# Norm factors by a block-diagonal matmul, and a gated-convolution loop interleaved slice by slice

## Chip, core and metric

The kernel runs on one core of a Trainium2 chip. The metric is device time in microseconds (us) of one execution. Beside it stands one profiled execution, whose trace gives the duration of every instruction and what each engine waited for.

## What is computed

```python
B, H, S, D = 8, 8, 576, 64          # DM = H * D = 512
kv  = einsum('bhsd,bhse->bhde', k, v)
out = einsum('bhsd,bhde->bhse', q, kv)
x   = out / sqrt(mean(out * out, -1) + 1e-6) * g_norm      # per head, 64 values
x   = x.transpose(0, 2, 1, 3).reshape(B, S, DM)
x1, x2, x3 = split(x @ w_proj, 3)                          # w_proj: 512 x 1536
x2  = irfft(rfft(x2, axis=1) * rfft(filter_fft, axis=0))   # along S, 576 long
result = (x1 * x2 * x3) @ w_out                            # 8 x 576 x 512, float32
```

## The kernel before

Everything is held transposed: the 512 channels lie on partitions as four **slices** of 128 (two heads each), the 576 rows of a batch along the free axis, as two halves of 288. Matmul operands are bf16, sums fp32.

The Fourier transforms are matmuls by tables that the kernel makes at its start (`ang`, `IV`, `FW`, `FWr`). The 576 rows are folded into three blocks of 192: `rr` is their sum, `ab` two differences. One transform of a batch is three groups: g = 0 on the sum (97 frequencies), g = 1 (128), and g = 2 (a middle piece). The transformed filter lies in `HH` and `HM`.

The work of one batch is written as functions:

- `kv(b)`: 40 matmuls for the k-v products of all heads, copied into `kvblk`; `qtr(b)`: 36 transposes of q, copied into `qT`.
- `att_o(b, j)`: two matmuls give slice j of the attention output. ScalarE (ACT) squares it into `sq`, and copies it times `g_norm` into `osb` (in batch 0 VectorE, DVE, does the copy).
- `att_r(b)`: eight matmuls by `ind_sq`, 32 columns wide, add the squares per head for all four slices into one tile; ACT makes Ln and Exp(-0.5 ...) of it, one each of 128x576, in `rstd`.
- `att_x(b, jp)`: matmuls by `ind_bc` spread the factors of a pair of slices over the 64 rows of each head, and DVE multiplies them from PSUM into `x`.
- `fold(b)`: three DVE operations over all four slices give `rr` and `ab`.
- `proj2(b)`: the x2 projection out of `rr` and `ab`; ACT copies it to `x2`.
- `fft(b)`: the three groups of the transform. DVE multiplies g = 0 and g = 1 twice each with `HH` (into `tpw`, 1024 elements), GpSimd (POOL) adds them into `Y`; g = 2 takes one DVE multiplication.
- `proj13(b, dc)`: sixteen matmuls for slice dc of x1 and x3. ACT copies x1, DVE multiplies x3 by it into `g13`.
- `invc`, `inv`: the inverse transform, folded; DVE combines its parts in four operations a pair of slices and multiplies with `g13` into `yg`.
- `outp(b)`: the output projection, copied by ACT and sent by DMA. The last 64 rows of two batches share a tile, so its third part runs for odd b only.

PSUM is one pool of four tiles (`psp`, bufs=4) of two banks each; every result above takes one. Most tiles in SBUF have one buffer: `x`, `ab`, `rr`, `qT`, `Y`, `g13`. Input loads are issued on POOL's queue, the filter and the outputs on SyncE's (SP's).

The order of the loop was: `proj2(b)`, `kv(b+1)`, `qtr(b+1)`, `fft(b)`, four times [`proj13(b, dc)`, `att_o(b+1, dc)`], `att_r(b+1)`, `outp(b-1)`, `att_x(b+1)`, `fold(b+1)`, `invc(b)`, `inv(b)`. A scheduler puts the instructions of each engine in a fixed order near to this one when the program is built; each engine then runs its own list in order and waits where an operand or a tile is not ready. Memsets without `tc.keep_in_program_order` may be put at any earlier place.

Of the kernel before, what the change touches and what calls it, by code (L numbers as in the profile page):

```python
# [20 lines left out]
def kernel(  # L21
# [26 lines left out]

    consts = ctx.enter_context(tc.tile_pool(name="consts", bufs=1))
# [64 lines left out]
    def load_filter():  # L114
        f4 = moe_filter_fft.rearrange("(m p c) d -> c p m d", m=3, c=3)
        lo, hi = slice(0, 64), slice(64, 128)
        for o, i in ((fa[lo, 0:3], f4[0]), (fa[hi, 0:3], f4[1]), (fa[lo, 3], f4[2][:, 1]), (fc[lo, 0], f4[2][:, 0]),
                     (fc[lo, 1], f4[2][:, 2]), (fc[hi, 0:2], f4[0][:, 1:3]), (fc[lo, 2:4], f4[1][:, 1:3]),
                     (fc[hi, 2:4], f4[2][:, 1:3])):
            nc.sync.dma_start(out=o, in_=i)  # L120
# [9 lines left out]
    for c, tag in enumerate(("x", "Y", "g13")):  # L130
# [9 lines left out]
        if c == 1:  # L140

            for t in (fa, fc):
                tc.keep_in_program_order(nc.vector.memset(t[:, :, 0:1], 0.0))
            load_filter()
# [14 lines left out]
    nc.vector.memset(bias_eps, 1e-6)  # L159


    ind_sq = consts.tile([P, 32], BF16)
    nc.vector.memset(ind_sq, 0.0)
    nc.vector.memset(ind_sq[0:64, 0:1], 1.0)
    nc.vector.memset(ind_sq[64:128, 1:2], 1.0)
    ind_bc = consts.tile([P, P], BF16)
    nc.vector.memset(ind_bc, 0.0)
    for j in range(4):
        nc.vector.memset(ind_bc[32 * j:32 * j + 2, 64:128], 1.0)
        nc.vector.memset(ind_bc[32 * j:32 * j + 1, 64:128], 0.0)  # L170
        nc.vector.memset(ind_bc[32 * j:32 * j + 1, 0:64], 1.0)
# [4 lines left out]
    def zeros(i):  # L176
        for t in kvt[i]:
            nc.vector.memset(t[TAIL:P], 0.0)
        nc.vector.memset(kvblk[i], 0.0)
# [68 lines left out]
    def att_r(b):  # L248
        s = st[b]
        r2 = ps_tile("ps_r2")  # L250
        for h in range(2):
            for j in range(NDC):
                nc.tensor.matmul(r2[32 * j:32 * j + 32, h, 0:TH], ind_sq, s['sq'][:, j, h * TH:(h + 1) * TH], start=True, stop=True)
        lr = work.tile([P, 2, TH], FP32, name="lr", tag="lr")
        nc.scalar.activation(out=lr, in_=r2[:, :, 0:TH], func=AF.Ln, scale=1.0 / D, bias=bias_eps)
        s['rstd'] = work.tile([P, 2, TH], BF16, name="rstd", tag="rstd")
        nc.scalar.activation(out=s['rstd'], in_=lr, func=AF.Exp, scale=-0.5)

    def att_x(b, jp):
# [3 lines left out]
        bc = [ps_tile("ps_bc") for _ in range(2)]  # L263
        for h in range(2):
            for i in range(2):
                r = slice(32 * (2 * jp + i), 32 * (2 * jp + i) + 32)
                nc.tensor.matmul(bc[i][:, h, 0:TH], ind_bc[r], s['rstd'][r, h], start=True, stop=True)  # L267
        for i in range(2):
            j = 2 * jp + i
            nc.vector.tensor_mul(out=s['x'][:, j].rearrange("p (a b) -> p a b", a=2), in0=bc[i][:, :, 0:TH],  # L270
                                 in1=s['o'][:, j].rearrange("p (a b) -> p a b", a=2))

    def fold(b):
        s = st[b]
        x3 = s['x'].rearrange("p j (m r) -> p j m r", m=3)
        ab = work.tile([P, NDC, 2, SB], BF16, name="ab", tag="ab")
        s['ab'] = ab.rearrange("p j a r -> p j (a r)")
        t_ = work.tile([P, NDC, SB], BF16, name="x01", tag="x01")
        s['rr'] = work.tile([P, NDC, SB], BF16, name="rr", tag="rr")
        nc.vector.tensor_add(out=t_, in0=x3[:, :, 0], in1=x3[:, :, 1])  # L280
        nc.vector.tensor_add(out=s['rr'], in0=t_, in1=x3[:, :, 2])
        nc.vector.tensor_sub(out=ab, in0=x3[:, :, 0:2, :], in1=x3[:, :, 2:3, :].to_broadcast([P, NDC, 2, SB]))
# [7 lines left out]
    def fold_filter():  # L290
        ff = hst['ff'] = work.tile([P, NSC, DM], BF16, name="ff", tag="x2")
        nc.vector.memset(ff[64:P, 1], 0.0)
# [9 lines left out]
        nc.vector.memset(asc, 2.0 / S)  # L302
        nc.vector.memset(asc[0:1, 0:1], 1.0 / S)
        nc.vector.memset(asc[96:97, 0:1], 1.0 / S)
# [45 lines left out]
    def fft(b):  # L350
        x2 = st[b]['x2']
        Y = work.tile([P, 6, DM], BF16, name="Y", tag="Y")
        st[b]['Y'] = Y
        for g in range(2):
            n = N1 if g == 0 else P
            ks = (0, 1) if g == 0 else (2, 3, 4)
            xp = ps_tile("ps_X")
# [7 lines left out]
        xp = ps_tile("ps_X")  # L365
# [56 lines left out]
    def outp(b):  # L422
        yg = yt[b % 2] = st[b]['yg']
        for c0 in (0, 2, 4):
            if c0 == 4 and b % 2 == 0:
                continue
# [13 lines left out]
            nc.scalar.copy(out=ot[:, 0:n], in_=pp[:, 0:n])  # L440
            for i in range(2):
                eng = nc.scalar if b == B - 1 and i else nc.sync
                if n == 2:
                    eng.dma_start(out=o_rows(b, 2 * c0 + i, 2 * c0 + 2 + i), in_=ot[64 * i:64 * i + 64])
                else:
                    eng.dma_start(out=o_rows(b - 1 + i, NR - 1), in_=ot[64 * i:64 * i + 64, 0])
# [3 lines left out]
    qtr(0)  # L450
    tables()
    for j in range(NDC):
        att_o(0, j)
    att_r(0)
    att_x(0, 0)
    att_x(0, 1)
    fold(0)
    fold_filter()
    for g in range(3):
        gen_h(g)  # L460
    zeros(1)
    for b in range(B):
# [5 lines left out]
        fft(b)  # L468
# [3 lines left out]
        for dc in range(NDC):  # L472
            proj13(b, dc)
# [45 lines left out]
```

## Time and profile before

| what | value |
|---|---|
| median of 3 runs | 278.64 us (277.81 to 281.88) |
| the profiled execution | 279.41 us, of which the span of its instructions is 277.6 us |
| granted TensorE clock, mean | 0.981 |
| busy: PE (TensorE) / DVE / ACT / POOL | 83% / 65% / 48% / 29% of the span |
| first matmul of batch 0's projection, of batch 1's, of batch 7's | 35.70, 67.12, 239.35 us |

The kernel is fully unrolled, so a batch can be read off the time line. In what follows "chain" is the chain of work that ended last, followed back from the end of the program; "groups" are instructions gathered by line and shape, with their number, total busy time, mean ns, and the idle time of the engine ahead of them with what ended it.

### The profile page before, as it was taken

How to read it: one execution, taken by the hardware profiler on the slowest of the kernel's cores; microseconds unless marked ns; L12 is line 12 of the kernel's file. 1: busy time of each engine (PE TensorE's matmuls, PEld its weight loads, DVE VectorE, ACT ScalarE, POOL GpSimd, SP SyncE). 2: the span in 40 equal slices, each digit the busy share in tenths (PEclk: the TensorE clock that was granted, in tenths of full speed). 3: DMA queues.
4: the chain of work that ended last, by engine and by line, in shares of the span. 5: the costliest groups of instructions: out<-in, count | busy, mean ns of one | idle time of the engine just before them, and what ended most of it. 6: DMA issues, size and time to landing. Idle time of an engine off the chain costs nothing.

```text
span 277.6 us, 4744 instructions
## 1 busy us (share of the span) xinstructions
PE 230.8 (83%) x1942; PEld 132.6 (48%) x1965; DVE 181.4 (65%) x283; ACT 133.6 (48%) x197; POOL 79.6 (29%) x80
## 2 busy tenths in 40 slices
PE   0227599959999899989998999999989999999690
PEld 0124125735575456545664556445744574466320
DVE  7909924739772998279936993499549952994520
ACT  1494255662367245834384437542773277233221
POOL 8722244800570058002910292003300230032000
PEclk9999999997999999999999999999999999999977
DMA  4999999990392529360985098510031002300506
GB/s 50 176 253 255 199 191 191 192 104 2 40 188 32 153 28 187 43 190 7 159 94 151 2 160 97 144 45 2 2 89 63 2 0 71 121 0 2 151 4 185
DMA packets 46231, 27.96 MB, mean 101 GB/s; under 512 B 22210, under 2 KB 40642, under 8 KB 46210
## 3 DMA queue, kind: packets, MB, share of 16 engines
q0 software_dynamic: 39744, 16.26, 48.5%
q1 hardware_dynamic: 6098, 10.75, 13.3%
q10 hardware_dynamic: 368, 0.66, 0.7%
q8 instruction: 15, 0.25, 0.3%
q14 instruction: 6, 0.05, 0.1%
HBM read 34.47 MB, written 9.44 MB: 158 GB/s over the span
## 4 chain that ended last, share of the span: by engine, by line
PE 68%; DVE 19%; issue 5%; DMA 3%; ACT 2%; ACTq 0%; SPq 0%; DVEq 0%
PE ps_x L379 22%; PE ps_out L432 10%; PE ps_x L346 8%; DVE x L270 6%; PE ps_X L360 6%; DMA fa<-in_moe_filter_fft_dram 3%; PE ps_qT L226 3%; DVE tpw L363 3%; PE ps_x L334 3%; PE ps_o L240 2%; PE ps_kv L211 2%; PE ps_inv L404 2%; PE ps_x L338 2%; PE ps_X L367 2%; PE ps_out L436 2%
## 5 line engine op out<-in xcount | busy, mean ns | idle before, releaser
L379 PE MATMUL ps_x<-x,wp 128*128 128x288 bf16 x512 | 67.5, 286 | 4.4 <-DVE tpw L363 4.4
L379 PEld LDWEIGHTS <-wp 128*128 128x128 bf16 x512 | 50.0, 98 | 19.8 <-issue 5.7
L364 POOL TENSOR_TENSOR Y<-tpw 97x1024 bf16<-97x1024 f32 (+1 forms) x16 | 37.6, 2358 | 72.7 <-DVE tpw L363 72.7
L270 DVE TENSOR_TENSOR x<-ps_bc,osb 128x576 bf16<-128x576 f32 x32 | 22.0, 749 | 30.2 <-PE ps_bc L267 30.2
L385 DVE TENSOR_TENSOR g<-ps_x,x 128x576 bf16<-128x576 f32 x32 | 24.0, 754 | 25.7 <-PE ps_x L379 25.7
L383 ACT CAST x<-ps_x 128x576 bf16<-128x576 f32 x32 | 20.4, 639 | 41.6 <-PE ps_x L379 41.6
L432 PE MATMUL ps_out<-wo,yg 128*128 128x512 bf16 x120 | 30.7, 389 | 2.8 <-DVE yg L413 2.4
L82 POOL DMA_DIRECT2D km<-in_k_dram x8 | 7.4, 924 | 82.9 <-PE ps_qT L226 78.0
L241 ACT ACTIVATE sq<-ps_o 128x576 bf16<-128x576 f32 x32 | 20.7, 650 | 17.5 <-PE ps_o L240 17.4
L440 ACT COPY ot<-ps_out 128x1024 f32<-128x1024 f32 (+1 forms) x20 | 18.3, 922 | 15.7 <-PE ps_out L432 14.9
L404 PE MATMUL ps_inv<-IV,Y 128*128 128x384 bf16 x128 | 23.4, 339 | 0.0
L346 PE MATMUL ps_x<-wp,ab 128*128 128x512 bf16 x96 | 22.1, 380 | 0.0
L229 DVE COPY qT<-ps_qT 128x512 bf16<-128x512 bf16 (+1 forms) x32 | 13.2, 452 | 12.4 <-PE ps_qT L226 11.9
L340 ACT CAST x<-ps_x 128x1024 bf16<-128x1024 f32 x8 | 8.1, 1015 | 27.1 <-PE ps_x L338 27.1
L246 ACT ACTIVATE osb<-ps_o,g_col 128x576 bf16<-128x576 f32 x28 | 20.6, 734 | 0.0
L432 PEld LDWEIGHTS <-yg 128*128 128x128 bf16 x128 | 11.5, 99 | 17.8 <-issue 3.0
L362 DVE TENSOR_TENSOR tpw<-ps_X,HH 97x1024 f32<-97x1024 f32 (+1 forms) x16 | 19.5, 1219 | 0.2
L363 DVE TENSOR_TENSOR tpw<-ps_X,HH 97x1024 f32<-97x1024 f32 (+1 forms) x16 | 19.4, 1213 | 0.0
L409 DVE TENSOR_TENSOR u<-ps_inv,cs 128x768 bf16<-128x768 f32 x16 | 15.2, 949 | 4.7 <-PE ps_inv L404 4.7
L360 PE MATMUL ps_X<-x,FW 128*128 128x512 bf16 (+1 forms) x57 | 17.9, 389 | 0.4
L226 PE MATMUL ps_qT<-ident,qb 128*64 128x128 bf16 x288 | 11.9, 232 | 6.3 <-DVE qT L229 4.0
L211 PE MATMUL ps_kv<-vm,km 128*64 128x64 bf16 x256 | 6.9, 203 | 12.2 <-DMA vm<-in_v_dram 12.2
(143 smaller groups left out, 321.9 us busy)
## 6 DMA issues: line engine op xcount, KB each, us to landing
out_dram<-ot SPq DMA_DIRECT2D x30, 256.0 KB, 3.4
qb<-in_q_dram POOLq DMA_DIRECT2D x16, 288.0 KB, 8.5
km<-in_k_dram POOLq DMA_DIRECT2D x8, 512.0 KB, 6.2
vm<-in_v_dram POOLq DMA_DIRECT2D x8, 512.0 KB, 8.1
wp<-in_moe_w_proj_dram POOLq DMA_DIRECT2D x3, 512.0 KB, 18.6
out_dram<-ot SPq DMA_DIRECT2D x7, 128.0 KB, 3.5
fa<-in_moe_filter_fft_dram SPq DMA_DIRECT2D x2, 384.0 KB, 8.2
fc<-in_moe_filter_fft_dram SPq DMA_DIRECT2D x3, 256.0 KB, 10.9
```

What stands on the lines that cost most here:

```text
L241: nc.scalar.activation(out=s['sq'][:, j].rearrange("p (a b) -> p a b", a=2), in_=op[:, :, 0:TH], func=AF.Square)
L246: nc.scalar.activation(out=o_, in_=op[:, :, 0:TH], func=AF.Copy, scale=g_col)
L270: nc.vector.tensor_mul(out=s['x'][:, j].rearrange("p (a b) -> p a b", a=2), in0=bc[i][:, :, 0:TH], in1=s['o'][:, j].rearrange("p (a b) -> ...
L346: nc.tensor.matmul(pp[:, cc], ab[:, j, (c0 + cc) * P:(c0 + cc + 1) * P], wp[:, j, DM:2 * DM], start=(j == 0), stop=(j == NDC - 1))
L360: nc.tensor.matmul(xp[:n, ri], FWr[:, ri, 0:n] if c == 1 else FW[:, a, 2 * g + ri, 0:n], x2[:, c], start=(a == 0), stop=(a == len(ks) - 1))
L363: nc.vector.tensor_mul(out=t_[:n, 1], in0=xp[:n], in1=HH[:n, g, 0:2])
L364: nc.gpsimd.tensor_add(out=Y[:n, 2 * g:2 * g + 2], in0=t_[:n, :, 0], in1=t_[:n, :, 1])
L379: nc.tensor.matmul(pp[:, h, 0:TH], w_, x[:, j, h * TH:(h + 1) * TH], start=(j == 0), stop=(j == NDC - 1))
L383: nc.scalar.copy(out=x1, in_=pp[:, :, 0:TH])
L385: nc.vector.tensor_mul(out=st[b]['g13'][:, dc].rearrange("p (a b) -> p a b", a=2), in0=pp[:, :, 0:TH], in1=x1)
L404: nc.tensor.matmul(ip[:, i, 0:2 * SB], Y[:, g, d_], IV[:, g, 0:2 * SB], start=(g == 2), stop=(g == 5))
L432: nc.tensor.matmul(pp[:, cc], yg[:, dc, c * P:(c + 1) * P], wo[:, dc], start=(dc == 0), stop=(dc == NDC - 1))
```

## The change

- `att_r` now runs per slice: two matmuls by a full 128x128 block-diagonal matrix `ind` give each row's sum already spread over its head's 64 rows. ACT takes Ln per slice and Exp per pair of slices, and `rstd` has the full 128x4x576 shape in SBUF. The matmuls of `att_x` are gone; its DVE multiplication takes both operands from SBUF, 1152 elements at a time.
- `fold` works on a pair of slices, so six DVE operations instead of three.
- The loop over slices now holds one transform group (in the order g = 1, 0, 2), `att_o`, `proj13`, `att_r`, and after each second slice `att_x` and `fold`. `outp(b-1)` follows after all of it.
- The first of `outp`'s copies goes to DVE.
- The last batch has its own ending, `last`: the inverse transform in one piece by six table rows (48 matmuls of 288 columns), one DVE multiplication a slice, and the output projection summed up slice by slice in three PSUM tiles.
- At the start: the sine table set of ACT is loaded first; the filter's load is issued in another place; batch 0's attention is slice by slice; `gen_h` runs inside batch 0, behind `kv(1)` and `qtr(1)`; most memsets keep their program order.

```diff
+    nc.scalar.preload_act_table_set("trig_and_small")
...
     def load_filter():
+        for t in (fa, fc):
+            tc.keep_in_program_order(nc.vector.memset(t[:, :, 0:1], 0.0))
...
+    ind = consts.tile([P, P], BF16)
+    tc.keep_in_program_order(nc.vector.memset(ind, 0.0))
+    for h in range(2):
+        tc.keep_in_program_order(nc.vector.memset(ind[64 * h:64 * h + 64, 64 * h:64 * h + 64], 1.0))
...
-    def att_r(b):
+    def att_r(b, j):
...
         for h in range(2):
-            for j in range(NDC):
-                nc.tensor.matmul(r2[32 * j:32 * j + 32, h, 0:TH], ind_sq, s['sq'][:, j, h * TH:(h + 1) * TH], start=True, stop=True)
...
+            nc.tensor.matmul(r2[:, h, 0:TH], ind, s['sq'][:, j, h * TH:(h + 1) * TH], start=True, stop=True)
+        nc.scalar.activation(out=s['lr'][:, j % 2].rearrange("p (a b) -> p a b", a=2), in_=r2[:, :, 0:TH], func=AF.Ln,
+                             scale=1.0 / D, bias=bias_eps)
+        if j % 2:
+            nc.scalar.activation(out=s['rstd'][:, j - 1:j + 1], in_=s['lr'], func=AF.Exp, scale=-0.5)
...
+        r = slice(2 * jp, 2 * jp + 2)
+        nc.vector.tensor_mul(out=s['x'][:, r], in0=s['o'][:, r], in1=s['rstd'][:, r])
...
+            if c0 == 0:
+                nc.vector.tensor_copy(out=ot, in_=pp)
+            else:
+                nc.scalar.copy(out=ot[:, 0:n], in_=pp[:, 0:n])
...
+    def last(b):
...
+        for dc in range(NDC):
+            ip = ps_tile("ps_inv")
+            for g in range(6):
...
+                    nc.tensor.matmul(ip[:, h, 0:TH], Y[:n, g, dc * P:(dc + 1) * P], IV[:n, g, h * TH:(h + 1) * TH],
+                                     start=(g == 0), stop=(g == 5))
...
+            if dc:
+                part(dc - 1)
+        part(NDC - 1)
+        for c in range(NSC):
...
+                (nc.scalar if i else nc.sync).dma_start(out=o_rows(bb, blk), in_=ot[64 * i:64 * i + 64, 0])
...
     kv(0)
     qtr(0)
+    load_filter()
     tables()
...
-        fft(b)
+        if b == 0:
+            for g in (1, 0, 2):
+                gen_h(g)
...
         for dc in range(NDC):
+            if dc < 3:
+                fft(b, (1, 0, 2)[dc])
+            if nxt:
+                att_o(b + 1, dc)
             proj13(b, dc)
             if nxt:
-                att_o(b + 1, dc)
-        if nxt:
-            att_r(b + 1)
+                att_r(b + 1, dc)
+                if dc % 2:
+                    att_x(b + 1, dc // 2)
+                    fold(b + 1, dc // 2)
         if b:
-            outp(b - 1)
+            for c0 in (0, 2, 4):
+                outp(b - 1, c0)
             del st[b - 1]
-        if nxt:
-            att_x(b + 1, 0)
-            att_x(b + 1, 1)
-            fold(b + 1)
+        if not nxt:
+            last(b)
+            continue
         invc(b)
```

How the order of instructions moves is seen at three places. In the lists a name's end number is one tile's; `ps_x` is the tile of a projection, `ps_r` of `att_r`, `ps_X` of a transform group, `ps_o` of `att_o`.

First TensorE in the loop over slices, batch 1. Before, all transform groups come first, and a slice is x1, x3, then the next batch's attention:

```order
L367 MATMUL ps_X<-x_725,FW 128x512
...
L379 MATMUL ps_x_871<-x,wp 128x288
...
L379 MATMUL ps_x_882<-x,wp 128x288
...
L240 MATMUL ps_o<-qT,kvblk_174 128x288
...
L379 MATMUL ps_x_899<-x,wp 128x288
```

Of the change, the same place one batch later:

```order
L353 MATMUL ps_X<-x_1062,FW 128x512
...
L233 MATMUL ps_o<-qT,kvblk_152 128x288
...
L372 MATMUL ps_x_1201<-x,wp 128x288
...
L372 MATMUL ps_x_1212<-x,wp 128x288
...
L250 MATMUL ps_r_1224<-sq,ind 128x288
...
L353 MATMUL ps_X<-x_1062,FW 97x512
```

A slice now takes five PSUM tiles of the four: a transform, the attention, x1, x3, and the sum of squares; the next transform stands behind them.

Second ScalarE in two slices of the same loop. Before, Ln (L255) and Exp (L257) stand behind the fourth slice:

```order
L383 CAST x_934<-ps_x_925 128x576
L241 ACTIVATE sq<-ps_o 128x576
L246 ACTIVATE osb<-ps_o,g_col 128x576
L383 CAST x_960<-ps_x_951 128x576
L241 ACTIVATE sq<-ps_o 128x576
L246 ACTIVATE osb<-ps_o,g_col 128x576
L255 ACTIVATE lr<-ps_r_977,bias_eps 128x576
L257 ACTIVATE rstd<-lr 128x576
```

Of the change:

```order
L234 ACTIVATE sq<-ps_o 128x576
L239 ACTIVATE osb<-ps_o,g_col 128x576
L376 CAST x_1210<-ps_x_1201 128x576
L251 ACTIVATE lr<-ps_r_1224,bias_eps 128x576
L234 ACTIVATE sq<-ps_o 128x576
L239 ACTIVATE osb<-ps_o,g_col 128x576
L376 CAST x_1251<-ps_x_1242 128x576
L251 ACTIVATE lr<-ps_r_1263,bias_eps 128x576
L254 ACTIVATE rstd<-lr 128x1152
```

Each slice now has a Ln, each second one an Exp twice as long, ahead of the next slice's square.

Third the start. VectorE before: the filter's tiles are touched (L143, after which SP issues the filter's load) between the angle computations, and its first use (L294) stands ahead of the copies of q:

```order
L137 TENSOR_TENSOR ang<-ang 128x576 x2
L143 MEMSET fa 128x4
L143 MEMSET fc 128x4
L134 TENSOR_SCALAR ang<-tv,kcol 128x576
L135 TENSOR_SCALAR ang<-ang 128x576
L136 TENSOR_SCALAR ang<-ang 128x576
L137 TENSOR_TENSOR ang<-ang 128x576
L294 TENSOR_TENSOR t_349<-fa 128x512
L229 COPY qT<-ps_qT 128x4x2x64 x2
```

Of the change:

```order
L171 MEMSET kt_83 64x256
L171 MEMSET vt_84 64x256
L172 MEMSET kvblk_151 128x256
L222 COPY qT<-ps_qT 128x4x2x64 x2
L222 COPY qT<-ps_qT 128x5x2x64 x2
L118 MEMSET fa 128x4
L118 MEMSET fc 128x4
L186 COPY FW<-ps_ft 128x640
```

The copies of q no longer stand behind the filter, and the filter's load is behind them. On TensorE the first k-v products of batch 1 now stand inside batch 0's x2 projection, where they came behind all of it before:

```order
L326 MATMUL ps_x_349<-wp,rr 128x512
...
L338 MATMUL ps_x_369<-wp,ab 128x512
...
L204 MATMUL ps_kv<-vm_82,km_81 64x64
...
L338 MATMUL ps_x_359<-wp,ab 128x512
...
L330 MATMUL ps_x_349<-wp,rr 64x512
```

So whatever holds up batch 1's k or v now also holds the rest of that projection.

132 lines of the change are left out of this document (65 added, 67 removed).

## Prediction

> **What bounds the kernel now.** I read the page first, then the span cut at the first projection matmul of batches 0, 1 and 7, then the chain and the time line of one middle batch.
>
> ```profile
> PE 230.8 (83%) x1942; PEld 132.6 (48%) x1965; DVE 181.4 (65%) x283; ACT 133.6 (48%) x197; POOL 79.6 (29%) x80
> ```
>
> ```profile
> 67.55:95.77 28.22, 26.44 (x235) 15.47 (x238) 19.28 (x27) 14.83 (x22) 9.36 (x8) 1.00 0.67 101
> ...
> 35.70:67.55 31.85, 28.01 (x235) 16.39 (x239) 17.51 (x24) 16.50 (x27) 12.27 (x12) 0.95 1.19 142
> 239.79:277.60 37.81, 27.79 (x157) 14.83 (x158) 18.56 (x25) 10.30 (x13) 4.67 (x2) 0.91 0.21 63
> ```
>
> Columns: length, then busy time of PE, PEld, DVE, ACT, POOL, the granted clock, the DMA share. There are three parts: a start of 35.7 us, seven like batches, and a last batch of 37.8. In a middle batch PE is busy 26.4 of 28.2 us, DVE 19.3, ACT 14.8: PE is the bound, and a gain can come only from PE's waits, the start and the end. The chain shows where PE waits (start, length, what):
>
> ```profile
> 75.92 0.43 PE ps_X L367 x2
> ...
> 78.00 1.14 DVE tpw L363
> ...
> 81.55 1.96 PE ps_x L379 x16
> ...
> 85.96 0.23 PE ps_r L253 x3
> ...
> 86.94 0.35 PE ps_r L253 x5
> 87.29 2.91 PE ps_out L432 x13
> 90.20 0.40 PE ps_bc L267 x6
> ...
> 95.77 0.59 PE ps_x L334 x2
> ```
>
> ```profile
> 91.64 0.83 PE L392 MATMUL ps_c<-IV,Y 97*128 97x192 bf16 x8
> 92.31 2.77 PE L404 MATMUL ps_inv<-IV,Y 128*128 128x384 bf16 x16
> ```
>
> First wait: the gate matmuls wait for the transforms' tiles; the group row of L379 below has 4.4 us over seven batches, 0.63 each. Second: the output ends at 90.20, the broadcast matmuls take 0.40, yet `invc` (L392) begins at 91.64: 1.04. Third: `inv` ends at 95.08, but the projection runs freely only from 95.77, since `rr` is late: some 0.6. With 0.2 of small change that is **2.5 us a batch**; 25.7 are work.
>
> **The steady batches.** The rows that I use (mean ns; idle time ahead, with what ended it):
>
> ```profile
> L379 PE MATMUL ps_x<-x,wp 128*128 128x288 bf16 x512 | 67.5, 286 | 4.4 <-DVE tpw L363 4.4
> L432 PE MATMUL ps_out<-wo,yg 128*128 128x512 bf16 x120 | 30.7, 389 | 2.8 <-DVE yg L413 2.4
> ...
> L270 DVE TENSOR_TENSOR x<-ps_bc,osb 128x576 bf16<-128x576 f32 x32 | 22.0, 749 | 30.2 <-PE ps_bc L267 30.2
> L241 ACT ACTIVATE sq<-ps_o 128x576 bf16<-128x576 f32 x32 | 20.7, 650 | 17.5 <-PE ps_o L240 17.4
> L246 ACT ACTIVATE osb<-ps_o,g_col 128x576 bf16<-128x576 f32 x28 | 20.6, 734 | 0.0
> L383 ACT CAST x<-ps_x 128x576 bf16<-128x576 f32 x32 | 20.4, 639 | 41.6 <-PE ps_x L379 41.6
> L413 DVE TENSOR_TENSOR yg<-u,g 128x1152 bf16<-128x1152 bf16 x16 | 12.1, 758 | 0.5
> L362 DVE TENSOR_TENSOR tpw<-ps_X,HH 128x1024 f32<-128x1024 f32 x8 | 9.7, 1214 | 0.0
> L348 ACT CAST x<-ps_x 128x1024 bf16<-128x1024 f32 x8 | 8.1, 1018 | 5.7 <-PE ps_x L346 5.7
> L255 ACT ACTIVATE lr<-ps_r,bias_eps 128x576 f32<-128x576 f32 x8 | 5.9, 740 | 1.1 <-PE ps_r L253 0.7
> L257 ACT ACTIVATE rstd<-lr 128x576 bf16<-128x576 f32 x8 | 5.5, 682 | 0.3
> L280 DVE TENSOR_TENSOR x<-x 128x768 bf16<-128x768 bf16 x8 | 4.4, 556 | 0.2
> ```
>
> PE loses `ind_sq` (0.23 + 0.35) and `ind_bc` (0.40), 0.98; it gains eight full matmuls of 288 columns at 1.96/16 = 0.122, also 0.98. Net nothing.
>
> DVE loses four multiplications of 0.749 and gets two of 1152 elements; L413 has that shape and type at 0.758: minus 1.5. Halving `fold` adds three instructions; a half costs more than half of L280's 0.556 and less than all of it, 0 to 0.8 in all, I take 0.4. The output copy is not in the trace on DVE: above 0.4 (two copies of q, 512 columns each, take 0.75 at 21.84 below), and by L362 about 1.2; I take 1.2. DVE stays near 19.4.
>
> ACT gets three more Ln (2.2), and two Exp of 1152 elements for one of 576: each between 0.68 and 1.36, by L348's 1.018 for 1024 1.15, so plus 1.6; it loses one copy, 1.0. ACT goes to about 17.7 of 26, but most of it stands in the slice loop, so I walk that loop. PE per slice: a transform of 6, 4, 3, 0 matmuls at 0.215 (L367), attention 0.25, x1 and x3 1.96, squares 0.25: 3.76, 3.3, 3.1, 2.46, together 12.6. DVE per slice: two multiplications of 1.21 and one of 0.75, 3.2, in slices 0 and 1; less in 2 and 3. ACT: 0.65 + 0.73 + 0.64 + 0.74 = 2.8, and 3.9 where an Exp follows.
>
> So DVE just keeps up, and ACT falls behind once. Counted from the loop's first matmul, PE ends slice 1 at 7.1 and slice 2 at 10.2. ACT's Ln and Exp of slice 1 (L251, L254) end at 9.1; queued behind them are the square, the scaled copy and the x1 cast of slice 2, which end near 9.75, 10.5 and 11.1. Slice 3 on PE takes over the tiles that the copy and the cast give back: it waits 0.3 for the one and, after its attention, 0.3 for the other. I charge **0.5** new wait a batch. The bounds: 0, if ACT makes it up, since in L383's row it has 41.6 us of waiting for PE over the run; 2.4, if ACT sets the pace throughout (rival B).
>
> Do the three old waits go? Transforms lie 3 us apart now, and the tile of one is needed five tiles later, when its 2.4 us of DVE are over. The broadcast tiles are gone. `rr`: `x` has one buffer, so DVE's first `x` of batch b+1 waits for the last x3 matmul of b, and behind it queue the last gate product, both folds, the second `x` and the output copy: 0.76 + 0.75 + 1.25 + 0.76 + 1.2 + 1.25 = 6.0. In that time PE has 0.25 of squares, 3.5 of output (16 at 0.224), 3.3 of `invc` and `inv`: 7.0. Covered with 1 us left; if that cover were gone, `rr` would be late again. In batch 0, without output, 0.45 is late. Saved per batch 2.5 - 0.5 = 2.0; from 67.55 to 239.79 are six batches: **12.0 us**.
>
> **The start.**
>
> ```profile
> 5.17 0.13 DVE L122 CAST kcol<-ki 128x3 f32<-128x3 int32 x1
> 10.71 0.68 ACT L138 ACTIVATE ang<-ang 128x576 f32<-128x576 f32 x1 [8.68 <-DVE ang L137]
> 11.39 1.97 SPq L120 DMA_DIRECT2D fa<-in_moe_filter_fft_dram  x3
> 11.41 1.28 ACT L146 ACT_TABLE_LOAD   x1
> 14.49 0.88 POOL L82 DMA_DIRECT2D vm<-in_v_dram  x1 [0.46 <-DMA qb<-in_q_dram]
> 20.59 0.74 ACT L215 CAST kvblk<-ps_kv 64x256 bf16<-64x256 f32 x2
> 21.84 0.75 DVE L229 COPY qT<-ps_qT 128x512 bf16<-128x512 bf16 x2
> ```
>
> ```profile
> vm<-in_v_dram POOLq DMA_DIRECT2D x1, 512.0 KB, 23.9
> ```
>
> Memsets held the first cast until 5.17; behind the tables, they free up to 2.8 us, and the table load of 1.28 goes: `kvblk` is ready near 17.2 instead of 21.3. The copies of q no longer wait for the filter. Batch 0's attention begins about 4 us earlier, near 20, and its first pair of slices is folded near 27. But batch 1's v, issued at 14.49, landed 23.9 later, at 38.4 (last row: size, us to landing), and the new order has the first k-v products of batch 1 inside this projection: PE stops there. The loads are one stream and DMA is full (share 1.19 in batch 0's row), and the filter's bytes, issued near 19.8 instead of 11.4, landing some 10 us after, go through the same engines before 38, so v comes no later and hardly earlier. From 38.4: 2.8 for the rest of the projection, 0.6 k-v, 1.1 transposes, 3.5 filter transform (ten full matmuls at 0.224, twelve half ones at 0.1), and a slow clock:
>
> ```profile
> 62.19 1.23 PE ps_c L392 x8
> 63.42 3.87 PE ps_inv L404 x16
> ```
>
> ```profile
> 63.40:67.30 3.90, 3.90 (x18) 1.99 (x16) 3.84 (x7) 0.80 (x1) 0.00 (x0) 0.68 0.00 0
> ```
>
> The chain has DVE and ACT ahead of 62.19: PE had waited for the factors and then for `x`, 2.4 us in two pieces. Then it was granted 0.68, and `inv` took 3.87 us (from 63.42) where a batch later it takes 16 x 0.164 = 2.62: 1.25 lost. I charge this once, since PE idles some 8 us before 38.4. Then 47.7 for the first transform, 12.6 + 0.5 slices, 3.3 + 0.45: batch 1's projection at 64.6 instead of 67.1: **2.5 us**. Bounds: 0 (1.3 if the clock is slow twice as long), and 6 if v lands early.
>
> The Trainium skill, TensorE: Matmul & The Clock Gate, "HAM oscillation", puts the drop to half clock at gaps of more than about 3.4 us. By it the clock would have stayed up at 63; the row shows a drop after shorter gaps, and the measurement decides. By Part 1 of that page, half rate for a window of 3.4 us costs 1.7, so the sum below would be 0.45 longer.
>
> **The last batch.**
>
> ```profile
> 263.45 1.55 PE ps_out L432 x4
> ...
> 269.32 0.72 ACTq L444
> ...
> 271.08 0.59 ACT ot L440
> ```
>
> `last` does the inverse in 48 matmuls at 0.122, 5.9, for 3.3 now: plus 2.6. The wait for `yg` that ends at 263.45 (2.4 in L432's row) goes, since each slice's product lies under the next slice's matmuls. At the end ACT copied, issued (269.32), and after its last copy (271.08, 0.59) issued once more, to 272.4: 4.1 us from the end of PE's work at 268.3. Now it copies three times 0.59 and issues five DMAs at 0.72, 5.4, of which 0.8 lie beside the last matmuls: 4.6. Sum **plus 0.7** (2.6 - 2.4 + 0.5), within 2 either way.
>
> **Sum.** 12.0 + 2.5 - 0.7 = 13.8 off. The profiled execution took 279.41 (span 277.6), so 265.6; it lies 0.8 above the median of 278.64, from which I count: 264.8.
>
> **Rivals.**
> B, ACT paces the slices: slices with an Exp take 3.9 + 0.4 of hand-overs, the others 2.8 + 0.4: 15.0 instead of 12.6. Five tiles a slice out of four make PE wait for whichever reader is late. The 2.5 us are then spent again: 28.1 a batch, 277. For it: Ln and Exp stand ahead of each next square. Against: slices 0 and 2 leave ACT 1.0 and 0.3 of slack, and the last one has the output behind it. Halfway, 271. The Trainium skill, Perfetto Trace Analysis, "Identifying Performance Opportunities", reads a gap repeating on the saturated engine as too little PSUM; before, the 0.63 of L379 recurs in seven batches, as it says; the change keeps four tiles.
> C, the start stays: the filter, issued 8 us later, holds the folds and the filter transform until 42, so batch 1 starts as now: 267.
> D, slower: each transform's tile is needed before DVE is through. One exposed multiplication of 1.21 in three slices and one Exp of 1.15 make 4.8 new waits for 2.5 old: plus 2.3 in seven batches, 295. It decides from 0.63 a slice on. For it: DVE needs 3.2 of a slice's 3.3; against: the tile is taken up again five tiles later.
> E, v lands early and no new wait remains: 12 + 3 (six batches without the 0.5) + 6 (the start's bound) - 0.7 off, 258.
>
> **Chances.** Forecast 0.57 (259 to 269), B 0.17, C 0.10, D 0.08, E 0.08. The range leaves out D, the far end of B and of E: 257 to 273. A measurement here tells 2%, 5.6 us, from no change. Faster by more (below 273): forecast, C, E and a third of B, 0.80; within: 0.12; slower: 0.08.
>
> **What would show it.** Right: middle batches of 26.2 us, no wait of a projection for `rr`, PE stopping at batch 1's first k-v until about 38, PE waits of 0.2 to 0.4 at slice 3 ended by ACT. Wrong: PE idle in each slice ahead of attention or x1 (B), ended by DVE's `tpw` (D); filter folds later than 42 (C). The forecast rests most on the four PSUM tiles being given back as I walked it, and on the landing of batch 1's v.

## The result and the profile after

The changed kernel took 268.98 us (median of 4 runs, 268.52 to 269.72) against 279.49 for the kernel before beside it: ratio 0.962, with an interval of 0.954 to 0.97. It is faster, by 10.5 us of the 13.8 that were forecast. Its profiled execution took 268.72, with a span of 267.0 (277.6 before). The ratios here and below are taken without the few executions that were slower as a whole, so a ratio need not be the quotient of two medians.

The same three views as before: the page's busy times; then the span by stages (length, then busy time of PE, PEld, DVE, ACT, POOL, the granted clock, the DMA share); then the chain of a middle batch (start, length, what).

```profile
PE 223.7 (84%) x1895; PEld 137.4 (51%) x1925; DVE 179.1 (67%) x283; ACT 150.6 (56%) x220; POOL 80.3 (30%) x80
```

```profile
68.22:228.43 160.21, 156.41 (x1375) 97.57 (x1398) 122.73 (x185) 104.95 (x153) 46.89 (x36) 1.00 0.53 85
121.82:147.89 26.07, 25.55 (x228) 16.13 (x229) 20.20 (x31) 17.17 (x25) 9.36 (x8) 1.00 0.73 108
228.43:267.00 38.57, 29.22 (x182) 17.07 (x183) 18.33 (x23) 7.83 (x11) 4.71 (x2) 0.95 0.29 80
```

Two of the rows above are cut at 228.43, where the chain has the last batch's first projection matmul; the matmul begins at 228.27. Counted from first matmul to first matmul in both kernels (67.12 and 239.35 before, 68.22 and 228.27 now), the stretch from batch 1's projection to batch 7's was 172.2 us and is 160.1: **12.2 less, 12.0 forecast**. Every second batch also has the third part of the output, which makes it 1.0 longer (28.2 and 29.2 before, 26.1 and 27.2 now). The row of one batch above has none of it, like the row ahead of the prediction: 26.07 for 28.2, where 26.2 was forecast, and ACT busy 17.17, where 17.7 was. The last batch has 38.7 for 38.3. What is missing lies ahead of 68.22, where batch 1 now starts; it started at 67.12 before, and 64.6 was forecast. The three parts, 12.2 - 0.5 - 1.1, are the 10.6 between the spans.

```profile
108.99 0.99 PE ps_x L372 x8
...
110.61 0.63 ACT osb L239
111.24 0.54 ACT x L376
...
111.82 2.12 PE ps_x L372 x16
...
119.39 2.60 PE ps_inv L397 x16
121.99 0.86 PE ps_x L326 x4
```

The chain leaves TensorE once in the batch, at slice 3, where ACT's scaled copy and x1 cast come late. `inv` runs straight into the next projection at 121.99; no broadcast and no `rr` stand between.

The start, from the chain of the same run and its stages:

```profile
15.04 24.93 DMA vm<-in_v_dram
...
40.10 0.43 PE ps_kv L204 x8
...
51.34 1.40 PE ps_X L353 x6
```

```profile
28.00:40.00 12.00, 1.48 (x4) 0.30 (x2) 7.17 (x15) 0.00 (x0) 2.24 (x3) 0.50 1.41 214
40.10:44.00 3.90, 3.90 (x18) 1.19 (x19) 0.00 (x0) 0.61 (x1) 1.49 (x2) 0.50 1.52 195
```

TensorE does 1.48 us of work in the twelve before v lands (its last wait, for v alone, is 10.6), and then 3.9 us at a granted clock of 0.50. The first transform runs at 51.34; 47.7 was forecast.

### The profile page after: what moved, and what is told of

Its sections match the earlier page's. It is cut to its first block, busy times and chain, and to the rows that moved or that the text cites. A ratio compares the mean times of both kernels' runs of the same rounds, so it can differ in the third digit from the quotient of the medians.

```text
span 267.0 us, 4694 instructions
## 1 busy us (share of the span) xinstructions
PE 223.7 (84%) x1895; PEld 137.4 (51%) x1925; DVE 179.1 (67%) x283; ACT 150.6 (56%) x220; POOL 80.3 (30%) x80
## 4 chain that ended last, share of the span: by engine, by line
PE 71%; DMA 13%; ACT 6%; DVE 4%; POOL 2%; issue 2%; ACTq 0%; POOLq 0%
PE ps_x L372 21%; DMA vm<-in_v_dram 9%; PE ps_out L423 9%; PE ps_X L353 6%; PE ps_x L338 6%; PE ps_inv L397 6%; DMA qb<-in_q_dram 3%; PE ps_qT L219 3%; PE ps_inv L459 2%; PE ps_x L326 2%; PE ps_o L233 2%; PE ps_r L250 2%; PE ps_X L360 2%; ACT osb L239 2%; PE ps_kv L204 2%
## 5 line engine op out<-in xcount | busy, mean ns | idle before, releaser
L357 POOL TENSOR_TENSOR Y<-tpw 128x1024 bf16<-128x1024 f32 (+1 forms) x16 | 37.8, 2361 | 74.7 <-DVE tpw L356 74.7
L251 ACT ACTIVATE lr<-ps_r,bias_eps 128x576 f32<-128x576 f32 x32 | 23.7, 745 | 6.5 <-PE ps_r L250 5.5
L355 DVE TENSOR_TENSOR tpw<-ps_X,HH 128x1024 f32<-128x1024 f32 (+1 forms) x16 | 19.6, 1224 | 9.4 <-PE ps_X L353 9.4
L423 PE MATMUL ps_out<-wo,yg 128*128 128x512 bf16 x106 | 25.0, 379 | 0.3
L338 PE MATMUL ps_x<-wp,ab 128*128 128x512 bf16 x90 | 23.8, 403 | 0.8 <-DVE ab L273 0.4
L204 PEld LDWEIGHTS <-km 128*64 128x64 bf16 x256 | 6.2, 119 | 26.4 <-issue 18.0
L356 DVE TENSOR_TENSOR tpw<-ps_X,HH 128x1024 f32<-128x1024 f32 (+1 forms) x16 | 19.4, 1215 | 0.0
L397 PE MATMUL ps_inv<-IV,Y 128*128 128x384 bf16 x112 | 19.4, 326 | 0.0
L261 DVE TENSOR_TENSOR x<-osb,rstd 128x1152 bf16<-128x1152 bf16 x16 | 12.1, 756 | 10.2 <-PE ps_x L372 9.9
L254 ACT ACTIVATE rstd<-lr 128x1152 bf16<-128x1152 f32 x16 | 18.6, 1165 | 0.5
L353 PE MATMUL ps_X<-x,FW 128*128 128x512 bf16 (+1 forms) x58 | 17.7, 381 | 0.2 <-ACT x L340 0.2
L402 DVE TENSOR_TENSOR u<-ps_inv,cs 128x768 bf16<-128x768 f32 x14 | 13.4, 954 | 6.2 <-PE ps_inv L397 6.2
```

The costliest lines, as they stand in the source:

```text
L251: nc.scalar.activation(out=s['lr'][:, j % 2].rearrange("p (a b) -> p a b", a=2), in_=r2[:, :, 0:TH], func=AF.Ln, scale=1.0 / D, bias=bias_eps)
L338: nc.tensor.matmul(pp[:, cc], ab[:, j, (c0 + cc) * P:(c0 + cc + 1) * P], wp[:, j, DM:2 * DM], start=(j == 0), stop=(j == NDC - 1))
L353: nc.tensor.matmul(xp[:n, ri], FWr[:, ri, 0:n] if c == 1 else FW[:, a, 2 * g + ri, 0:n], x2[:, c], start=(a == 0), stop=(a == len(ks) - 1))
L355: nc.vector.tensor_mul(out=t_[:n, 0], in0=xp[:n], in1=HH[:n, g, 1:3])
L357: nc.gpsimd.tensor_add(out=Y[:n, 2 * g:2 * g + 2], in0=t_[:n, :, 0], in1=t_[:n, :, 1])
L397: nc.tensor.matmul(ip[:, i, 0:2 * SB], Y[:, g, d_], IV[:, g, 0:2 * SB], start=(g == 2), stop=(g == 5))
```

## The experiments

Each run is compared with the kernel before; its median lay between 279.0 and 279.5 in all of them. The stages come from each run's profiled execution: the first matmul of batch 2's projection, the time from there to batch 7's (five batches), and from there to the end.

| kernel | median, us | ratio, interval | batch 2 starts | five batches | last batch |
|---|---|---|---|---|---|
| before | 279.49 | | 95.32 | 144.0 | 38.3 |
| changed | 268.98 | 0.962, 0.954 to 0.97 | 94.67 | 133.6 | 38.7 |
| norm factors only | 282.61 | 1.0136, 1.0096 to 1.0177 | 98.67 | 143.9 | 38.4 |
| order only | 267.34 | 0.9588, 0.9546 to 0.9629 | 89.99 | 138.2 | 37.1 |
| filter and projection first | 262.52 | 0.941, 0.9382 to 0.9438 | 88.37 | 133.6 | 38.7 |
| filter loaded early | 268.22 | 0.9586, 0.9533 to 0.9638 | 94.51 | 133.6 | 38.7 |
| wo last | 266.73 | 0.9569, 0.9537 to 0.9601 | 92.10 | 133.6 | 38.7 |
| five output buffers | 267.91 | 0.96, 0.9575 to 0.9626 | 95.03 | 133.6 | 38.1 |
| Exp later | 267.32 | 0.9589, 0.9557 to 0.9622 | 95.04 | 132.3 | 38.7 |
| first start and end together | 262.51 | 0.9408, 0.9387 to 0.9429 | 89.24 | 133.6 | 38.0 |
| end by two engines | 268.63 | 0.9666, 0.9606 to 0.9726 | 94.74 | 133.6 | 38.7 |
| best | 260.27 | 0.9356, 0.9272 to 0.9439 | 88.37 | 132.3 | 38.7 |
| old end | 268.08 | 0.9638, 0.9569 to 0.9707 | 94.25 | 133.6 | 39.1 |
| filled gap | 265.99 | 0.953, 0.9514 to 0.9545 | 92.63 | 133.6 | 38.8 |

### Which half of the change brings the middle batches' gain

Two kernels take the kernel before and do one half each. **Norm factors only**:

```diff
-            nc.tensor.matmul(r2[32 * j:32 * j + 32, h, 0:TH], ind_sq, ...)
+            nc.tensor.matmul(r2[:, h, 0:TH], ind, ...)      # Ln per slice, Exp per pair; order as before
```

> The kernel before with the new norm alone: full block-diagonal matmul, Ln per slice, Exp per pair of slices, factors from SBUF; all else, the order of the loop too, as before. Theory (three separate waits of 0.63, 1.04 and 0.6 us a batch make up the gain): only the wait of the broadcast matmuls (1.04) goes, the wait for the transforms' tiles stays, middle batches of 27.2 (without the odd third output part), about 272. Rival 1 (the norm brings nearly everything, since without the broadcast the fold comes early too): 26.2 a batch, about 266. Rival 2 (five more ACT operations behind the last slice make the fold as late as the broadcast did): no change, 278.

**Order only**, with the old norm factors, folds, start and ending:

```diff
-        fft(b)
         for dc in range(NDC):
-            proj13(b, dc)
+            if dc < 3:
+                fft(b, (1, 0, 2)[dc])
             if nxt:
                 att_o(b + 1, dc)
+            proj13(b, dc)
```

> The kernel before with the transforms interleaved with the slices (in the order g = 1, 0, 2) and attention ahead of the gates, nothing else: old norm, fold, output, start and end. Theory: the wait of the gate matmuls for the transforms' tiles (0.63 a batch) goes and nothing else, 27.6 a batch, about 275. Rival (interleaving alone lets PE run through): 26.2 a batch, about 266. Rival (five tiles a slice out of four cost as much as the old wait): no change.

TensorE's waits in the five middle batches, by what it waited for (us in total, times, longest). Before:

```profile
PE ps_x L379 <- DVE tpw L363: 3.1, 5, 0.6
PE ps_bc L267 <- ACT ot L440: 2.0, 5, 0.7
PE ps_x L334 <- DVE rr L281: 1.8, 5, 0.5
```

Order only:

```profile
PE ps_bc L267 <- ACT ot L441: 2.0, 5, 0.7
PE ps_x L334 <- DVE rr L281: 1.8, 5, 0.5
```

Norm factors only:

```profile
PE ps_x L370 <- DVE tpw L354: 3.2, 5, 0.6
PE ps_x L325 <- DVE rr L272: 3.1, 3, 1.0
PE ps_r L251 <- ACT osb L240: 1.5, 5, 0.3
PE ps_out L423 <- ACT lr L252: 1.1, 5, 0.2
PE ps_r L251 <- DVE g L376: 0.9, 5, 0.2
```

In the changed kernel this view names no wait in the same stretch. So of the three the order takes away the wait of the gate matmuls alone, and the norm factors the broadcast's alone; these bring new waits at the sums of squares and at the output, 3.5 in all. The third wait, for `rr`, goes with neither half. The whole change also has what neither half has, the folds by pairs and the first output copy on DVE; no run takes these apart, so which of them the third wait needs is not shown. With the old order, the chain of norm factors only shows what stands ahead of `rr`, behind the fourth slice:

```profile
90.06 1.27 ACT lr L252 x2
91.36 1.17 ACT rstd L255
92.55 1.37 ACT lr L252 x2
...
94.83 1.07 ACT rstd L255
...
98.06 0.56 DVE rr L272
```

Four Ln and two Exp, 4.9 us, stand here behind the last slice, with a copy of the output between them. The output and the inverse cover most of it, but in a batch without the third output part the next projection still waits 1.0 for `rr`. In the five batches the order alone saves 5.8 (3.1 is the wait named; the view gives no name to the rest), the norm factors alone 0.1, the whole change 10.4: what it adds to the order is worth 4.6, where the slices take the norm factors up one by one. By themselves the norm factors cost 3.5 us (ratio 1.0136), nearly all of it ahead of batch 2 (98.67 for 95.32): at the end of batch 0, with no output to cover them, the next projection waits 4.7 for `rr` and then runs at a clock of 0.54. The first expectation, 272, was wrong by 10.

The second, 275, was wrong by 8. Beside the middle batches, where the order saved 1.2 each instead of 0.63, order only starts batch 1 at 62.94 (4.2 earlier than before), and its last batch is 1.1 shorter; behind two waits that both kernels have, the clock dropped in the kernel before (0.68 from 63.4 on, 0.60 from 263 on) and stayed at 1.00 in this one. The order alone, at 267.34, is not slower than the whole change, and that points to the start.

### The start

**Filter and projection first**: the changed kernel, with the filter's transform and the whole x2 projection of batch 0 ahead of batch 1's k-v products.

```diff
         proj2(b)
-        if nxt:
-            kv(b + 1)
-            qtr(b + 1)
         if b == 0:
             for g in (1, 0, 2):
                 gen_h(g)
+        if nxt:
+            kv(b + 1)
+            qtr(b + 1)
```

> The change, but in batch 0 the filter's transform and all of the x2 projection stand on TensorE ahead of the first k-v product of batch 1 (held there by program order). Theory (the start is lost because PE stops at batch 1's first k-v product, until its v has landed near 40, with 5 us of ready work queued behind): that work fills the stop, the first transform starts near 45 instead of 51, about 263. Rival (the start is bound by the loads themselves, or by the filter's fold at 38): under 2 us gained, 267 to 269.

It is 6.5 us faster than the changed kernel, by the stages 6.3, all ahead of batch 2, and nothing else moved. Its chain reaches the first transform at 44.51, by way of the filter:

```profile
20.66 9.86 DMA fa<-in_moe_filter_fft_dram
...
43.55 0.92 ACT HM L320
...
44.51 0.38 PE ps_X L355
```

**Filter loaded early**, between the angle computations:

```diff
-    load_filter()      # behind qtr(0)
+        if c == 1:     # in the loop that computes ang
+            load_filter()
```

> The change, but the filter's load is issued where it was before (between the angle computations, near 9 instead of 20 us), so that its first use stands on VectorE ahead of the copies of q again. Theory (PE's stop for batch 1's v sets the start; loads are one stream, so v lands at about the same time whichever comes first, and the later attention is hidden by that stop): v lands between 38 and 40, 267 to 269. Rival (the late load of the filter costs the start): 3 us gained, 266. Rival (the attention of batch 0 sets the start): 4 us lost, 273.

It moves the start by 0.2 only. The filter is issued 12 us earlier, but q of batch 0 now lands 6.4 later (21.13 for 14.75), batch 0's projection begins at 36.8 for 26.98, and the k-v products still stand until v has landed, at 40.83.

```profile
6.51 14.62 DMA qb<-in_q_dram
...
21.42 19.41 DMA vm<-in_v_dram
```

**wo last**:

```diff
-    load_w(wo, moe_w_out)
     load_kv(1)
     load_q(1)
+    load_w(wo, moe_w_out)
```

> The changed kernel with one edit at the start: the load of the output projection's weights (wo, 512 KB, needed only behind batch 1's slices) is issued behind batch 1's k, v and q instead of ahead of them. Theory: the early loads share one saturated stream, so batch 1's v, for which TensorE stops inside batch 0's projection, lands earlier by wo's bytes: 512 KB at the 200 GB/s that the start moves are 2.6 us; v lands at about 37.4 instead of 39.97 and everything behind follows, 266.4 us against 269.0. Rival 1: the order of issue does not set the order of landing, v lands as late as before, 269. Rival 2: v comes early enough, but the filter's second part, folded at 38.3, takes its place as the last to arrive, 267.5.

```profile
13.15 24.01 DMA vm<-in_v_dram
...
37.29 0.42 PE ps_kv L204 x8
```

v lands at 37.15, 2.8 earlier, and batch 2 starts 2.6 earlier. Here the loads act as one stream, and what stands behind v follows it nearly one for one; the filter's second part did not take its place.

**Filled gap**: 46 matmuls of unused result keep TensorE at work until v lands.

```diff
+        if b == 0:
+            dm = ps_tile("ps_dm")
+            for _ in range(46):
+                nc.tensor.matmul(dm[:, 0], st[0]['ab'][:, 0, 0:P], wp[:, 0, DM:2 * DM], start=True, stop=True)
         proj2(b)
```

> The changed kernel with 46 matmuls (128x512, result unused) put ahead of batch 0's x2 projection: they fill the stretch in which TensorE waits for the filter's fold and batch 1's v. The projection now stands whole behind them, and batch 1's k-v products behind it. Theory: in the changed kernel the granted clock was 0.50 from 27 until 44, so the 4 us of matmuls behind the wait ran at half rate and lost 2.0; with TensorE kept busy the clock is 1.00 when v lands near 40 and batch 1 starts 2 us earlier, 267.0 us against 269.0. Rival 1: the casts of ScalarE and the tiles that they free pace this stretch (0.9 us of the chain), so at most 1 comes back, 268. Rival 2: the clock stays at half through dense work too, the 46 matmuls take 20 us and the kernel is slower, 276.

```profile
28.00:32.00 4.00, 4.00 (x11) 1.36 (x9) 1.47 (x3) 0.00 (x0) 0.68 (x1) 0.50 1.22 235
...
40.00:50.00 10.00, 10.00 (x121) 4.77 (x119) 1.65 (x4) 5.88 (x11) 5.10 (x7) 1.00 1.59 192
```

```profile
39.83 0.86 PE ps_x L326 x4
...
49.61 0.54 PE ps_X L353 x2
```

Useless work makes the kernel 3.0 us faster by the medians (in the trace batch 2 starts 2.0 earlier). The clock is 0.50 at first (row of 28 to 32, TensorE busy throughout), 0.93 from 32 to 36, and 1.00 when v lands. The whole projection now starts at 39.83, six of its matmuls later than in the changed kernel, and yet the first transform comes at 49.61 for 51.34, at a clock of 1.00. The half clock was the cost of having waited, more than the casts of ACT in this stretch were, from which at most 1 was expected back. The run also takes batch 1's k-v out of the projection; v has landed by then, so this should not matter, but it was not run apart.

### ScalarE in the slices

**Exp later**: the Exp of slices 0 and 1 stands behind the x1 cast of slice 2 (and `lr` has a second buffer, so that the next Ln need not wait for it).

```diff
-                    att_x(b + 1, dc // 2)   # behind att_r of slice 1, with its Exp
+                if dc == 2:
+                    rs(b + 1, 1)            # the Exp of slices 0 and 1, kept in this place
+                    att_x(b + 1, 0)
+                    fold(b + 1, 0)
```

> The changed kernel with one ScalarE instruction moved: the Exp of the first pair of slices (1.16 us) stands behind the x1 cast of slice 2 instead of ahead of that slice's square; the DVE multiplication and the folds that need it move with it. No work is added or removed. Theory: the new wait of 0.54 us a batch at slice 3 (TensorE held by ScalarE's scaled copy and x1 cast) is ScalarE being late by that Exp; moved, the wait goes in seven batches: 3.8 us off, 265.2 us. Rival 1 (ScalarE paces the slices in any order): the same wait turns up one slice later, ahead of the output's first tile, 269. Rival 2: the later factors delay the first multiplication into x, and the sum of blocks (rr) is late again, 0.5 a batch more, 272.

TensorE in the same slices, timeline (start, length):

```profile
111.40 0.41 PE L233 MATMUL ps_o<-qT,kvblk 128*128 128x288 bf16 x2
111.65 2.12 PE L378 MATMUL ps_x<-x,wp 128*128 128x288 bf16 x16
113.61 0.41 PE L250 MATMUL ps_r<-sq,ind 128*128 128x288 bf16 x2
114.13 3.61 PE L429 MATMUL ps_out<-wo,yg 128*128 128x512 bf16 x15
```

The wait at slice 3 is gone, and half of it turns up ahead of the output: 113.61 + 0.24 would be 113.85, and the output starts at 114.13. Five batches take 1.3 less, 0.27 each, and the kernel 1.7. So the wait was ACT being late by that Exp, and about half of it can be had back by the order: theory and first rival each hold in part.

### The end

**Five output buffers** in the last batch:

```diff
-            ot = work.tile([P, 2, DM], FP32, name="ot", tag="ot", bufs=3)
+            ot = work.tile([P, 1, DM], FP32, name="ol", tag="ol", bufs=5)
```

> The changed kernel with one edit at the end: the five output copies of the last batch have five buffers of their own instead of sharing three. Theory: in the changed kernel the fourth and fifth copy wait 2.0 us until an earlier tile has been sent; with five buffers the end comes 2.0 us earlier, 267.0 us against 269.0. Rival: the sends themselves (five, two queues) set the end and only the copies move: 269.

The changed kernel's chain at the end:

```profile
258.65 2.02 DMA out_dram<-ot
...
262.07 0.58 ACT ot L472
```

The 2.02 of waiting for a sent tile go, but only 0.7 of the last batch comes back. Timeline with five buffers:

```profile
257.70 0.59 ACT L472 COPY ol<-ps_out 128x512 f32<-128x512 f32 x1 [9.23 <-PE ps_out L450]
...
258.32 0.69 DVE L470 COPY ol<-ps_out 128x512 f32<-128x512 f32 x1 [1.60 <-ACT ol L472]
259.76 0.59 ACT L472 COPY ol<-ps_out 128x512 f32<-128x512 f32 x1 [1.47 <-DVE ol L470]
```

The copies take turns: DVE's waits for ACT's copy of the same tile, and ACT's next stands behind the issue that sends what DVE copied. **End by two engines** gives each engine a tile:

```diff
+        nc.scalar.copy(out=ots[0], in_=po[0])
+        nc.vector.tensor_copy(out=ots[1], in_=po[1])
+        nc.scalar.copy(out=ots[2][:, 0], in_=po[2][:, 0])
```

> The changed kernel with its last copies regrouped: ScalarE copies the whole first output tile (128x1024) and then the fifth block, DVE the whole second tile beside it; ScalarE sends two of the six transfers, after its copies, SyncE four. Theory: in the run with five buffers the copies still took turns, since two engines read one tile one after the other and ScalarE's queue held its next copy behind sending what DVE had copied; with a tile for each engine the copies are over 1.65 us after TensorE's end at 257.3, SyncE's four issues of 0.7 end at 261.2 where the last one now ends at 263.2: 2.0 off, 267.0 us. Rival: four issues on one queue and larger transfers (256 KB) take back what the copies give: 268.5 or more.

```profile
257.41 1.01 ACT L467 COPY ot<-ps_out 128x1024 f32<-128x1024 f32 x1 [9.23 <-PE ps_out L450]
...
257.84 1.23 DVE L468 COPY ot<-ps_out 128x1024 f32<-128x1024 f32 x1 [1.41 <-PE ps_out L450]
...
259.83 2.79 SPq L474 DMA_DIRECT2D out_dram<-ot  x2
```

The copies are over at 259.07 instead of 262.65, and the span still ends at 267.1: SyncE's last two issues now take 0.9 and 1.8 (2.79 together), where 0.7 each was expected. The rival held. The traces point at the sends: in the changed kernel, five output buffers, end by two engines and old end alike, the DMA engines move the last 1.3 MB between 259 and 265 (busy share 0.8 to 1.0 from 260 to 264 in end by two engines), and the span ends some 2 us behind them. No run sends less at the end, so this is not shown.

**Old end**: the last batch as every other one.

```diff
-        if not nxt:
-            last(b)
-            continue
+    for c0 in (0, 2, 4):      # behind the loop
+        outp(B - 1, c0)
```

> The changed kernel without the new ending: the last batch does its inverse transform and output projection as every other batch does (folded inverse, combined by DVE, three output parts). Theory: the new ending costs more on TensorE (48 matmuls for 24, plus 2.6) than it saves in waits and copies; the kernel with the new order and the old ending took 37.1 us from the last batch's first projection matmul to the end where the changed kernel takes 38.6: 1.4 off, 267.6 us. Rival (the prediction's own sum, plus 0.7 for the new ending): 268.3. Rival 2: without the new ending the wait for the inverse's combination, 2.4, comes back in full: 270.5.

The last batch takes 39.1 for 38.7, the medians 268.1 and 269.0 with overlapping ranges: no difference that could be told. The expectation had taken 37.1 from the order-only run. In both kernels TensorE waits 2.40 us for the inverse's combination (the figure in brackets; old end first), but behind it the old end got about half the clock here (first row, 252 to 256) and the order-only kernel the full one:

```profile
252.31 0.61 PE L423 MATMUL ps_out<-wo,yg 128*128 128x512 bf16 x1 [2.40 <-DVE yg L406]
```

```profile
252.61 1.04 PE L433 MATMUL ps_out<-wo,yg 128*128 128x512 bf16 x4 [2.40 <-DVE yg L414]
```

```profile
252.00:256.00 4.00, 3.48 (x10) 1.02 (x12) 2.02 (x4) 0.00 (x0) 0.00 (x0) 0.57 0.01 3
```

```profile
252.00:256.00 4.00, 3.35 (x17) 1.28 (x18) 2.33 (x4) 0.04 (x1) 0.00 (x0) 1.00 0.00 0
```

At full clock the 3.48 us of work in the first row would take about 2.0 (3.48 x 0.57, an estimate), so without the drop the old end would be some 1.5 shorter: which ending is better hangs on the clock, and is not settled.

### Put together

**First start and end together** is filter and projection first, with wo last and the five buffers.

> The kernel with the filter transform and the whole x2 projection of batch 0 ahead of batch 1's k-v products (262.5 us measured), with the edits of the two runs above: wo loaded behind batch 1's inputs, and five output buffers in the last batch. Theory: the end gives 2.0; the start gives up to 1.5 more, since q of batch 1 landed at 43.5, just ahead of the first transform at 44.5, which then waits for the filter alone: 259.5 us. Rival: with the waits for loads gone the filter's chain (landing at 30.5, folds, transform, scaled copies until 44.4) still sets the start, 260.5. Rival 2: nothing adds up, 262.5.

The end gives 0.7, but the start loses 0.9, and the second rival held. The chain of the start goes through the filter, which waits for its issue behind batch 0's transposes, and those for q of batch 0; the filter lands at 30.83 here and at 30.52 without the two edits, and the last matmuls of the x2 projection then take 0.6 longer (1.71 for 1.16).

**Best** has, on filter and projection first, wo last, the Exp later, the end by two engines, and the filter's fold held behind both folds of batch 0:

> The kernel with the filter transform and the whole x2 projection of batch 0 ahead of batch 1's k-v products (262.5 us measured), and: wo loaded last, the Exp behind the x1 cast of slice 2, the end by two engines, and DVE's fold of the filter held behind both folds of batch 0 (in that kernel DVE waited for the filter until 30.5 with the second multiplication into x queued behind it). Theory: the second pair of slices is folded near 29 instead of 34, the x2 projection ends near 35, the filter's transform and its scaled copies near 42, and the first transform runs at 42 instead of 44.5; with 1.7 from the Exp and 2.0 from the end: 256.3 us. Rival: ScalarE's seven scaled copies of the filter (4.1 us) still follow the fold of a filter that lands at 30.5, the start gains at most 1: 258. Rival 2: the gains do not add, 260.

It is the fastest kernel of this study, 260.27, 8.7 us below the changed one and ratio 0.9356 to the one before. Over filter and projection first it gains 2.3 by the medians and 1.4 by the spans of the two profiled executions (260.7 and 259.3), all of it in the middle batches; 256.3 was expected, and the second rival held. Batch 2 starts at 88.37 in both. Holding the fold did free the projection (ACT begins its last casts at 34.61 for 38.03), but then q of batch 1 came last, at 42.50:

```profile
19.57 22.93 DMA qb<-in_q_dram
```

## Why the prediction was right, and which term was not

- **The bound, and the three waits.** TensorE was the bound, and its waits were the gain. The first has been shown to go by the order and the second by the norm factors; the third goes in the whole change and with neither half. The sizes of the parts were not the forecast's: the order alone saved 1.2 a batch, where its wait was priced at 0.63.
- **2.0 us a batch.** 12.0 were forecast for six batches and 12.2 measured. TensorE's work did not grow (busy 223.7 for 230.8). The DVE chain behind `inv`'s cover, forecast at 6.0, is 5.2: the first `x` starts at 113.97, and the last `rr` ends at 119.2, while the next projection begins at 121.82. `rr` is no longer late.

```profile
113.97 0.76 DVE L261 TENSOR_TENSOR x<-osb,rstd 128x1152 bf16<-128x1152 bf16 x1 [1.42 <-PE ps_x L372]
...
118.86 0.35 DVE L272 TENSOR_TENSOR rr<-x,x 128x384 bf16<-128x384 bf16 x1
```

- **The new wait of 0.5** is there, at slice 3, ended by ACT; Exp later shows its cause. Rival B (ACT paces the slices) does not hold, though ACT could give back only half of the wait.
- **The estimates for operations not in the trace**: DVE's output copy, 1.2, took 1.22; the Exp of 1152 elements, 1.15, took 1.17; the multiplication, 0.758, took 0.756.
- **The start is the step that failed**, in the term "2.5 us": measured, batch 1 starts 1.1 later, a miss of 3.6. The mechanism was right, and the sizes were not. TensorE stops at batch 1's first k-v products inside the projection until v lands, and from the first transform to batch 1's projection it took 16.9, the 12.6 + 0.5 + 3.3 + 0.45 of the forecast. Two sizes were off. v began to be used at 40.1, not 38.4 (1.7): "so v comes no later and hardly earlier" took the landing from the old order. And from there to the first transform were 11.2, not 9.3 (1.9): one slow stretch of 1.25 was charged, where 3.9 us ran at a clock of 0.50, which loses 2.0, and casts and tiles were waited for behind it. Filled gap shows the second (the first transform 1.7 earlier with the clock up), and wo last that the first goes nearly one for one into the whole (v 2.8 earlier, batch 2 2.6).
- **The other rivals.** C's time, 267, is near the measured one, but its mechanism is not the cause: the filter was not the last to arrive (wo last). E's start comes near with the stop gone instead of v early: filter and projection first starts batch 1 at 61.71, 5.4 earlier than before, where E had 6. D's exposed multiplications do not occur; no wait ends on them.
- **What the working did not ask** is whether the stop had to be there. Against the old start under the new order (order only, batch 1 at 62.94), the changed start costs 5.3 us (68.22); with batch 1's k-v behind the projection it gains 1.2 (61.71). A stop seen in the order of instructions was priced, and accepted as part of the change, but its price was set against the old kernel's wait and not against the same kernel without it.
- **The last batch**, plus 0.7, is plus 0.5 (38.73 for 38.25) by the profile. The forecast had three copies of ACT in a row and five issues; the copies in fact take turns, and wait 2.0 for buffers. The size came out near with another composition, which is luck.
- **The clock.** The forecast weighed the rule of the Trainium skill, TensorE: Matmul & The Clock Gate, "HAM oscillation", that gaps of more than about 3.4 us halve the clock. Half rate behind a wait of 10.6 us agrees with it, but the clock was down from 28 on already, behind a wait of 2.58 for batch 0's `rr`. The end does not agree either: after a wait of 2.40 us the granted clock was 0.57 in old end and 1.00 in order only, so a drop can come behind a gap well below that length, and the length of the gap alone does not tell which of two equal waits it follows. What does was not found.

## To carry to other kernels

Chains of small operations that shorten the way (here norm factors without a broadcast) are worth something only where they are spread under another engine's work; in one piece at the end of the loop the same operations brought nothing in the middle batches (0.1 in five) and cost 3.5 us ahead of them. Where the order of instructions shows the busiest engine stopping at a load inside work that is already ready, price the stop against the same kernel with those instructions moved behind that work, and add the slow clock that follows a long wait to its price. And a load that is not needed yet costs its bytes to the loads behind it (v 2.8 earlier without the 512 KB of `wo` ahead), on another queue too (q of batch 0, issued by POOL, 6.4 later beside SyncE's early filter).

## What the hardware showed that was not expected

- The granted clock was 0.50 from 28 to 44 us in the changed kernel, through twelve us with 1.5 of work and then 3.9 of dense work; with 46 matmuls of no use from 27.00 on it was 0.50 from 28 to 32, 0.93 from 32 to 36 and 1.00 after, and they paid for themselves (3.0 us).
- The same wait of 2.40 us was followed by a clock of 0.57 in one kernel and 1.00 in another.
- Copies of two halves of one PSUM tile by ACT and DVE ran one after the other (258.32 behind 257.70 + 0.59), and of two tiles side by side (257.84 within 257.41 + 1.01). The trace puts DVE's wait in the first down to ACT's copy; whether the program's own waits or the chip ask for it was not tried.
